# Half of the second weights split before the routing, and the routing table's one-hots on two engines, in an attention and two-MoE kernel

## The chip, the cores and the metric

The kernel runs on one core of a Trainium2 chip. Its time is device time in microseconds of one execution of the whole program. Of the version before there are three timed runs and one profiled execution. All times of a view count from the start of the profiled execution's span.

## What is computed

Three stages in fp32, each feeding the next:

```python
# 1: attention, 2 batches x 8 heads x 768 tokens x 64; a query sees the keys of its own cluster
scores = np.where(mask, scale * np.matmul(q, k.transpose(0, 1, 3, 2)), -1e9)
attn = softmax(scores); x = np.matmul(attn, v)          # then 1536 rows of 512
# 2: a mixture of 8 experts, two experts per row
noisy_logits = x @ w_gate + np.log1p(np.exp(x @ w_noise)) * noise
top2 = np.argpartition(-noisy_logits, 2, axis=1)[:, :2]
h = np.maximum(x[mask] @ w1[e], 0.0)                    # 512 -> 1024
out[mask] += top2_w[mask, k, None] * (h @ w2[e])        # 1024 -> 512
# 3: a second mixture of 8 experts, one expert per row, at most 384 rows each
expert_idx = np.argmax(logits, axis=1)
```

## The kernel before, in words

Everything runs in an order that the program writes out; each engine takes its instructions in that order. Each fp32 operand of a large matmul is split into a high and a low part (fp32r), and three products (high x high, high x low, low x high) make up one. ScalarE makes the high part by a copy, VectorE the low part by a subtraction. A weight half (w1 or w2 of one expert, 512x1024) arrives in four chunks of 512 KB through a staging ring of four buffers; `wload` (L179) queues the chunks, `op` (L199) splits one, `wstep` takes the next in the queue. The first weight half of all is split by ScalarE and GpSimd during attention. High and low part of a half stand in two tiles of a ring of three (`WB`); two of these three pairs are allocated only after attention has given its memory back (L1462).

Attention goes over 16 heads of 6 query tiles. Each head is summed in two halves (`av`, L807): twelve matmuls into one accumulator, which ScalarE then copies to `oT` (L825). `xback` (L829) turns the sums back, scales the rows (L842), writes them to memory, and adds the gate sums `lt` to `LG` (L844, L846).

The experts' work is a list of jobs. Job 0 takes the first expert's rows of batch 0, job 1 the same expert's rows of batch 1, then follow the other experts. A job's first layer is eight groups `wide1` (L1096, f = 0 to 7) of 12 matmuls, each emptied by ScalarE (`hh`, L1108) and VectorE (`hl`, L1109); three accumulators rotate. Its second layer (`second`, L1146) is one pass of 24 matmuls per tile of 128 rows, over eight chunks f. Then the next job's rows, which GpSimd gathers from memory (L1044), are transposed (L1085) and split (L1087, L1088).

Job 0 needs only batch 0. Job 1 needs to know which rows of batch 1 go to the first expert, and that is `route1(1)` (L360): it starts from the complete `LG` (L366), finds the two best experts (mask `A`, L395), sums ranks with small matmuls (`ranks`, L294), turns them to slots (L404 to L314), makes twelve pairs of one-hots (`one_hot`, L318: position `ohp` and value `ohv`, both on VectorE, four buffers each), adds twelve matmuls of them up to a table (L447), and makes the destinations and tokens of it (L449 to L337). Then the gather can be issued. `route1(1)` is a generator that runs beside job 0: at each pause of the job (`tick`, L996) it is advanced by as many steps as the numbers PA and K0 to K3 allow. So its instructions stand between those of job 0, on the same engines. In job 0 a split of the second weights is put behind every second group (L1311).

Of the kernel before, what the change touches and what calls it, by code (L numbers as in the profile page):

```python
# [26 lines left out]
def kernel(  # L27
# [39 lines left out]
    F0, FP, T0, PA = 1, (2, 4), 1.5, 3.0  # L67
    K0, K1, K2, K3 = 10, 3, 1.5, 2
# [104 lines left out]
    WB = [[ring.tile([128, 4096], F32R, name=f"w{p}0") for p in "hl"]]  # L173
# [5 lines left out]
    def wload(n):  # L179
# [5 lines left out]
        for g in range(4):  # L185
# [11 lines left out]
            cs = slice(g * 1024, (g + 1) * 1024)  # L197

            def op(cs=cs, raw=raw, g=g):  # L199
                wh, wl = WB[buf]  # L200
                W[n] = [w.rearrange("p (c f) -> p c f", c=nch) for w in (wh, wl)]
                nc.scalar.activation(wh[:, cs], raw[0], AF.Copy)  # L202
                nc.vector.tensor_tensor(wl[:, cs], raw[0], wh[:, cs].bitcast(F32), op=OP.subtract)  # L203
                clock["out"] -= 1
                wfill()

            def part(half, cs=cs, raw=raw, g=g):
                wh, wl = WB[buf]
                W[n] = [w.rearrange("p (c f) -> p c f", c=nch) for w in (wh, wl)]
                src = raw[0][:, half * 512:(half + 1) * 512]  # L210
                o = slice(cs.start + half * 512, cs.start + (half + 1) * 512)
                nc.scalar.activation(wh[:, o], src, AF.Copy)
                nc.gpsimd.tensor_tensor(wl[:, o], src, wh[:, o].bitcast(F32), op=OP.subtract)
# [146 lines left out]
    def route1(b, psum):  # L360
        LG = LGs[b]
        eng = nc.vector if b else nc.gpsimd
        z = LG[:, :, 8:16]
# [43 lines left out]
        yield  # L407
# [3 lines left out]
        yield  # L411
        t = rt.tile([128, 2, J, E], F32, name="st")
        nc.vector.tensor_tensor(t, oh, rkb[:, None, :, :].to_broadcast([128, 2, J, E]), op=OP.mult)
        yield
        s = rt.tile([128, 2, J], F32, name="ss")
        nc.vector.tensor_reduce(s, t, axis=AX.X, op=OP.add)
        yield
# [5 lines left out]
        yield  # L423
        f = yield from split_slots(s2[:, 0:2].rearrange("p a j -> p (a j)"), 2 * J, "sf")
# [1351 lines left out]
```

## Time and profile before

| what | value |
|---|---|
| timed runs, us | 853.73, 857.37, 858.87 (median 857.37) |
| profiled execution, us | 849.86 |
| its span, us | 848.1 |
| TensorE busy | 820.2 us, 97% |
| TensorE weight loads | 733.6 us, 87% |
| VectorE, ScalarE, GpSimd busy | 540.1, 495.1, 287.9 us |
| mean granted TensorE clock | 0.997 |

The profiled execution's own time is its span and 1.76 us around it. A busy share is a mean over stages with different limits; what a wait costs has to be read in its own stage.

### The profile page before, as it was taken

How to read it: one execution, taken by the hardware profiler on the slowest of the kernel's cores; microseconds unless marked ns; L12 is line 12 of the kernel's file. 1: busy time of each engine (PE TensorE's matmuls, PEld its weight loads, DVE VectorE, ACT ScalarE, POOL GpSimd, SP SyncE). 2: the span in 40 equal slices, each digit the busy share in tenths (PEclk: the TensorE clock that was granted, in tenths of full speed). 3: DMA queues.
4: the chain of work that ended last, by engine and by line, in shares of the span. 5: the costliest groups of instructions: out<-in, count | busy, mean ns of one | idle time of the engine just before them, and what ended most of it. 6: DMA issues, size and time to landing. Idle time of an engine off the chain costs nothing. (4 is left out here: it accounts for less than half of the span.)

```text
span 848.1 us, 14830 instructions
## 1 busy us (share of the span) xinstructions
PE 820.2 (97%) x5350; PEld 733.6 (87%) x5350; DVE 540.1 (64%) x1104; ACT 495.1 (58%) x959; POOL 287.9 (34%) x488
## 2 busy tenths in 40 slices
PE   8999999999998989999999999999999999999997
PEld 6999999888987868989888897988997789888895
DVE  7998888889988666447444443536476548565370
ACT  7989889888888315435343343436254347555461
POOL 3565565667764031231302021124322122222210
PEclk9999999999999999999999999999999999999999
DMA  3125521411113034744644454438465529775250
GB/s 97 34 72 181 198 73 33 147 46 50 39 39 111 20 138 152 241 161 137 185 157 138 166 150 137 119 138 275 144 222 181 191 80 295 274 233 183 87 166 18
DMA packets 62181, 116.75 MB, mean 138 GB/s; under 512 B 13737, under 2 KB 25769, under 8 KB 62096
## 3 DMA queue, kind: packets, MB, share of 16 engines
q1 hardware_dynamic: 52832, 92.60, 34.4%
q0 software_dynamic: 9264, 23.06, 8.1%
q8 instruction: 47, 0.77, 0.4%
q14 instruction: 38, 0.31, 0.1%
HBM read 97.29 MB, written 23.74 MB: 143 GB/s over the span
## 5 line engine op out<-in xcount | busy, mean ns | idle before, releaser
L203 DVE TENSOR_TENSOR wl<-raw,wh 128x1024 fp32r<-128x1024 f32 x124 | 150.3, 1222 | 44.9 <-ACT wh L202 42.5
L1106 PE MATMUL l<-xh,wh 128*128 128x256 f32 (+1 forms) x508 | 156.0, 309 | 2.3 <-ACT xh L1087 0.9
L1106 PE MATMUL l<-xh,wl 128*128 128x256 f32 (+1 forms) x508 | 155.4, 308 | 0.2 <-DVE wl L203 0.2
L1106 PE MATMUL l<-xl,wh 128*128 128x256 f32 (+1 forms) x508 | 148.1, 307 | 0.0
L1151 PE MATMUL l<-wh,hh 128*128 128x512 f32 x328 | 134.9, 411 | 1.5 <-PEq L1343 0.5
L202 ACT ACTIVATE wh<-raw 128x1024 fp32r<-128x1024 f32 x124 | 129.0, 1054 | 7.9 <-DMA raw<-in_moe_w_dram 6.9
L1153 PE MATMUL l<-wh,hl 128*128 128x512 f32 x328 | 129.3, 394 | 0.0
L1152 PE MATMUL l<-wl,hh 128*128 128x512 f32 x328 | 129.0, 393 | 0.0
L1109 DVE SCALAR_TENSOR_TENSOR hl<-l,hh 128x256 fp32r<-128x256 f32 (+1 forms) x127 | 61.3, 484 | 98.6 <-ACT hh L1108 96.4
L1108 ACT ACTIVATE hh<-l 128x256 fp32r<-128x256 f32 (+1 forms) x127 | 55.0, 433 | 101.5 <-PE l L1106 99.6
L801 DVE TENSOR_TENSOR El<-et,Eh 128x384 fp32r<-128x384 f32 x192 | 99.7, 550 | 11.1 <-ACT Eh L800 8.1
L1106 PEld LDWEIGHTS l<-xh,wh 128*128 128x128 f32 x508 | 95.6, 188 | 5.8 <-issue 2.8
L1106 PEld LDWEIGHTS l<-xh,wl 128*128 128x128 f32 x508 | 95.4, 188 | 1.1 <-DVE wl L203 0.4
L769 DVE TENSOR_REDUCE nm<-st 128x1 f32<-128x768 f32 x96 | 91.3, 951 | 6.0 <-PE st L764 4.9
L1106 PEld LDWEIGHTS l<-xl,wh 128*128 128x128 f32 x508 | 93.7, 188 | 0.6
L800 ACT ACTIVATE Eh<-et 128x384 fp32r<-128x384 f32 x192 | 87.2, 493 | 10.5 <-PE et L795 10.2
L778 ACT ACTIVATE E<-st,nm 128x768 f32<-128x768 f32 x96 | 87.1, 907 | 7.6 <-DVE nm L769 7.6
L1195 POOL DMA_INDIRECT y_dram<-y,t1d x23 | 23.2, 1010 | 195.5 <-ACT y L1174 157.5
L1153 PEld LDWEIGHTS l<-wh,hl 128*128 128x128 f32 x328 | 61.6, 188 | 14.9 <-DVE hl L1123 0.3
L1151 PEld LDWEIGHTS l<-wh,hh 128*128 128x128 f32 x328 | 61.8, 188 | 14.6 <-issue 3.1
L795 PE MATMUL et<-identr,Er 128*128 128x128 f32 x576 | 70.9, 241 | 1.1 <-DVE El L801 1.0
L763 PE MATMUL st<-KB,QC 80*128 80x384 f32 x192 | 70.6, 367 | 1.2 <-ACT E L778 1.2
(331 smaller groups left out, 1527.5 us busy)
## 6 DMA issues: line engine op xcount, KB each, us to landing
raw<-in_moe_w_dram SPq DMA_DIRECT2D x128, 512.0 KB, 4.4
vraw<-in_v_dram SPq DMA_DIRECT2D x16, 192.0 KB, 2.5
x_dram<-xp SPq DMA_DIRECT2D x8, 384.0 KB, 3.2
out_dram<-xg SPq DMA_DIRECT2D x1, 3072.0 KB, 9.9
y_dram<-xg SPq DMA_DIRECT2D x1, 3072.0 KB, 9.9
part<-y_dram SPq DMA_DIRECT2D x12, 256.0 KB, 4.2
yt<-y_dram SPq DMA_DIRECT2D x12, 256.0 KB, 4.4
x_dram<-part POOLq DMA_DIRECT2D x12, 256.0 KB, 4.4
```

The lines of the kernel that those rows point to most:

```text
L202: nc.scalar.activation(wh[:, cs], raw[0], AF.Copy)
L203: nc.vector.tensor_tensor(wl[:, cs], raw[0], wh[:, cs].bitcast(F32), op=OP.subtract)
L763: nc.tensor.matmul(ps, st["QC", i][:64 + C, js], st["KB", i][:64 + C, cs], start=True, stop=False)
L769: nc.vector.tensor_reduce(nm, ps, axis=AX.XY, op=OP.max, negate=True)
L778: made = nc.scalar.activation(E, st.pop(("S", i, j))[:, :, :HW], AF.Exp, bias=st.pop(("nm", i, j)), accum_out=st["Z", i][:, j:j + 1])
L795: ins = nc.tensor.transpose(ps[:, n * 128:(n + 1) * 128].bitcast(F32R), E[:, part, n * 128:(n + 1) * 128], identr)
L800: nc.scalar.activation(Eh[o], ps, AF.Copy)
L801: nc.vector.tensor_sub(El[o], ps, Eh[o].bitcast(F32))
L1106: nc.tensor.matmul(ps[:, :n], (w1l if k == 2 else w1h)[:, c, fs], (self.xl if k == 1 else self.xh)[:, c, :n], start=(m == 0), stop=(m == l ...
L1151: nc.tensor.matmul(ps[:rows], hh[:, f, cs], w2h[:, f, :], start=(f == 0), stop=False)
L1152: nc.tensor.matmul(ps[:rows], hh[:, f, cs], w2l[:, f, :], start=False, stop=False)
L1153: nc.tensor.matmul(ps[:rows], hl[:, f, cs], w2h[:, f, :], start=False, stop=(f == FC - 1))
```

## The change

The weight ring's two tiles of a half are cut the other way: tile a holds high and low part of the chunks 0 and 1, tile b those of 2 and 3. The first half-size tile of the second buffer now stands in the ring that exists during attention. So two of the four chunks of job 0's second weights are split before the routing: one before and one behind job 0's first group, which itself is put between the two halves of the last head. The other two are split inside the routing. Job 0's second layer goes by turns (`second_turns`): chunks f 0 to 3 for both tiles, then the twelve table matmuls, then 4 and 5, then 6 and 7. The rank matmuls come after group 5 (`FR`), the routing has fewer pauses, each one-hot has a buffer of its own, and of each pair's second choice ScalarE makes the value: Square of the distance, then Relu of code - 2 code x distance. In the last `xback` the gate sums come before the rows and stay on VectorE.

```diff
-    F0, FP, T0, PA = 1, (2, 4), 1.5, 3.0
-    K0, K1, K2, K3 = 10, 3, 1.5, 2
+    F0, FP, T0, PA, FR = 1, (2, 4), 1.5, 4.5, 5
...
-    WB = [[ring.tile([128, 4096], F32R, name=f"w{p}0") for p in "hl"]]
+    class Half:
+        def __init__(self, tiles, k, nch):
+            self.tiles, self.k, self.per = tiles, k, nch // 2
+        def __getitem__(self, key):
+            _, c, fs = key
+            w = self.tiles[c // self.per][:, self.k].rearrange("p (c f) -> p c f", c=self.per)
+            return w[:, c % self.per, fs]
+    def wtile(pool, p, n):
+        return pool.tile([128, 2, 2048], F32R, name=f"w{p}{n}")
+    WB = [[wtile(ring, p, 0) for p in "ab"], [wtile(ring, "a", 1)]]
...
-                wh, wl = WB[buf]
+                wh, wl = [WB[buf][g // 2][:, p, cs] for p in range(2)]
-                nc.scalar.activation(wh[:, cs], raw[0], AF.Copy)
-                nc.vector.tensor_tensor(wl[:, cs], raw[0], wh[:, cs].bitcast(F32), op=OP.subtract)
+                nc.scalar.activation(wh, raw[0], AF.Copy)
+                nc.vector.tensor_tensor(wl, raw[0], wh.bitcast(F32), op=OP.subtract)
...
-    def one_hot(f, n, code, ncol):
-        oh = rt.tile([128, 128], F32R, name="ohp", bufs=4)
+    def one_hot(f, n, code, ncol, pool=None, minus=None):
+        pool, k = (pool, 2 * J) if pool else (my, 4)
+        oh = pool.tile([128, 128], F32R, name="ohp", bufs=k)
         nc.vector.tensor_scalar(oh, lane, f[:, 0, n:n + 1], None, op0=OP.is_equal)
-        val = rt.tile([128, ncol], F32R, name="ohv", bufs=4)
+        val = pool.tile([128, ncol], F32R, name="ohv", bufs=k)
+        if minus is not None:
+            far = pool.tile([128, ncol], F32, name="far", bufs=2)
+            nc.scalar.activation(far, lane[:, :ncol], AF.Square, scale=-1.0, bias=f[:, 1, n:n + 1])
+            nc.scalar.activation(val, far, AF.Relu, scale=minus, bias=code)
+            return oh, val
...
+        if b:
+            minus = hot.tile([128, J], F32, name="minus")
+            nc.gpsimd.tensor_scalar(minus, code1[:, b, :, 1], -2.0, None, op0=OP.mult)
...
-        if b:
-            yield K0
+        while b and st["f"] < FR:
+            yield
         ps = psum()
         ranks(ps, A, 0)
-        if b:
-            yield K1
...
-            for j in range(J + 1):
-                if j < J:
-                    hots += [one_hot(f, c * J + j, code1[:, b, j, c:c + 1], NC1) for c in range(2)]
-                    yield K2
-                for c in range(2 if j else 0):
-                    n = 2 * (j - 1) + c
-                    nc.tensor.matmul(ps2[:, :NC1], *hots[n], start=(n == 0), stop=(n == 2 * J - 1))
-            yield K3
+            wneed0(1)
+            for j in range(J):
+                hots += [one_hot(f, c * J + j, code1[:, b, j, c:c + 1], NC1, hot, minus[:, j:j + 1] if c else None) for c in range(2)]
+            for n in range(2 * J):
+                while st["pairs2"] < 1:
+                    yield
+                nc.tensor.matmul(ps2[:, :NC1], *hots[n], start=(n == 0), stop=(n == 2 * J - 1))
             nc.vector.tensor_add(st["tab0"], ps2[:, :NC1], st["tab0"])
-            yield
-            st["dst1"], st["tok1"] = yield from finish_table(st["tab0"], "t1", True)
+            st["dst1"], st["tok1"] = drain(finish_table(st["tab0"], "t1", True))
+            wneed0(1)
+            yield
...
+        for part in (gates, rows) if i == NBH - 1 else (rows, gates):
+            part()
...
+        def second_turns(self, hh, hl, pause, before):
+            ps = [p2.tile([128, Dm], F32, name="l2") for _ in self.main]
+            for part, fs in enumerate(((0, 1, 2, 3), (4, 5), (6, 7))):
+                while sum(n == self.h + 1 for n, _, _ in wops) > 2 - part:
+                    wstep()
+                w2h, w2l = W[self.h + 1]
+                for t, rows in self.main:
+                    cs = self.cols(t, rows)
+                    for f in fs:
+                        nc.tensor.matmul(ps[t], hh[:, f, cs], w2h[:, f, :], start=(f == 0), stop=False)
+                        nc.tensor.matmul(ps[t], hh[:, f, cs], w2l[:, f, :], start=False, stop=False)
+                        nc.tensor.matmul(ps[t], hl[:, f, cs], w2h[:, f, :], start=False, stop=(f == FC - 1))
+                        if f % 2 == 1 and f < FC - 1:
+                            if (part, t, f) == (0, 1, 3):
+                                st["pairs2"] = 1
+                            elif (part, t) == (1, 0):
+                                st["pairs2"] = 2
+                            pause()
+                    if part == 2:
+                        y = my.tile([128, Dm], F32, name="y")
+                        nc.scalar.activation(y, ps[t], AF.Copy)
+                        before()
+                        self.scatter(t, rows, y)
+                        pause()
...
-            if (i, t, s) == (NBH, 1, 3):
+            if done[0] == 2 * NBH - 1 and "begun" not in st:
+                st["begun"] = True
                 wneed(0)
+                wneed0(1)
                 for f in range(F0):
                     jobs[0].wide1(f, *st["first"])
+                wneed0(1)
...
-    for n in (1, 2):
-        WB.append([ring3.tile([128, 4096], F32R, name=f"w{p}{n}") for p in "hl"])
+    WB[1].append(wtile(ring3, "b", 1))
+    WB.append([wtile(ring3, p, 2) for p in "ab"])
+    hot = phase["first"].enter_context(tc.tile_pool(name="hot", bufs=1, side="right", reuse_waits="tile"))
```

How the order moves, at three places. First VectorE where attention ends and the routing begins. Before (`hl` is the low part of job 0's first group, `z` the softmax scales, `ra` the routing's first tile):

```order
L801 TENSOR_TENSOR El<-et,Eh 128x3x128 x6
L1109 SCALAR_TENSOR_TENSOR hl<-st,hh 128x256
L832 TENSOR_SCALAR z<-Z 128x6
L833 RECIPROCAL z<-z 128x6
L842 TENSOR_TENSOR xp<-et,z 128x6x64
L844 TENSOR_TENSOR lt<-et,z 128x96
L366 SCALAR_TENSOR_TENSOR ra<-LG_104 128x48
```

Now:

```order
L829 TENSOR_TENSOR El<-et,Eh 128x3x128 x6
L218 TENSOR_TENSOR wa_112<-raw,wa_112 128x1024
L1144 SCALAR_TENSOR_TENSOR hl<-st,hh 128x256
L218 TENSOR_TENSOR wa_112<-raw,wa_112 128x1024
L860 TENSOR_SCALAR z<-Z 128x6
L861 RECIPROCAL z<-z 128x6
L876 TENSOR_TENSOR lt<-et,z 128x96
L878 TENSOR_TENSOR LG_104<-LG_104,lt 128x96
L873 TENSOR_TENSOR xp<-et,z 128x6x64
L390 SCALAR_TENSOR_TENSOR ra<-LG_104 128x48
```

Two weight splits (`wa`) stand ahead of the scales, and the gate sums `lt` and `LG` ahead of the row scaling `xp`.

Second, TensorE at the table matmuls (`ohv`, `ohp` are the one-hots; `l` with a number is a tile's accumulator of the second layer). Before:

```order
L1153 MATMUL l_4977<-wh_4793,hl 128x512
L447 MATMUL rps<-ohv,ohp 128x96 x6
L1151 MATMUL l_4977<-wh_4793,hh 128x512
L1152 MATMUL l_4977<-wl_4794,hh 128x512
L1153 MATMUL l_4977<-wh_4793,hl 128x512
L1151 MATMUL l_4977<-wh_4793,hh 128x512
L1152 MATMUL l_4977<-wl_4794,hh 128x512
L1153 MATMUL l_4977<-wh_4793,hl 128x512
L447 MATMUL rps<-ohv,ohp 128x96 x6
L1151 MATMUL l_5087<-wh_4793,hh 128x512
```

Now:

```order
L1225 MATMUL l_5060<-wa_112,hh 128x512
L1226 MATMUL l_5060<-wa_112,hl 128x512
L475 MATMUL rps<-ohv,ohp 128x96 x12
L1224 MATMUL l_5059<-wb_4798,hh 128x512
L1225 MATMUL l_5059<-wb_4798,hh 128x512
L1226 MATMUL l_5059<-wb_4798,hl 128x512
L1224 MATMUL l_5059<-wb_4798,hh 128x512
L1225 MATMUL l_5059<-wb_4798,hh 128x512
L1226 MATMUL l_5059<-wb_4798,hl 128x512
L1224 MATMUL l_5060<-wb_4798,hh 128x512
```

The two sixes, which stood before and behind the first tile's last two chunks, became one twelve, behind chunks 0 to 3 of both tiles.

Third, VectorE at the one-hots (`sf` holds the slots). Before:

```order
L310 TENSOR_SCALAR si<-si 128x12
L311 TENSOR_SCALAR si<-si 128x12
L314 CAST sf<-si 128x24
L321 TENSOR_SCALAR ohp<-lane,sf 128x128
L323 TENSOR_SCALAR ohv<-lane,sf,code_99 128x96
```

Now:

```order
L325 TENSOR_SCALAR si<-si 128x12
L326 TENSOR_SCALAR si<-si 128x12
L329 CAST sf<-si 128x24
L218 TENSOR_TENSOR wb_4798<-raw,wb_4798 128x1024
L336 TENSOR_SCALAR ohp<-lane,sf 128x128
L344 TENSOR_SCALAR ohv<-lane,sf,code_99 128x96
L336 TENSOR_SCALAR ohp<-lane,sf 128x128 x2
L344 TENSOR_SCALAR ohv<-lane,sf,code_99 128x96
```

A split (`wb`) stands between the slots and the first one-hot, and every second value is gone from VectorE. The two splits that stood ahead of the copy of the ranks (L404) are gone from there; the last of the four now stands behind the token table.

## Rows read from the trace of the kernel before

**Rows 1.** Stage windows: length, TensorE busy (instructions), granted clock, DMA share, GB/s.

```profile
293.57:312.45 18.88, 15.84 (x83) 1.00 0.13 39
312.45:323.95 11.50, 11.50 (x96) 1.00 0.84 302
338.00:450.00 112.00, 111.70 (x558) 1.00 0.54 173
```

**Rows 2.** TensorE timeline: start, us, line, operation [idle before <- releaser].

```profile
278.73 0.44 PE L822 MATMUL acc<-Eh,vt 128*128 128x384 f32 x1 [0.68 <-ACT oT L825]
...
282.40 0.36 PE L1106 MATMUL l<-xh,wh 128*128 128x256 f32 x1
...
290.65 0.39 PE L1106 MATMUL l<-xh,wh 128*128 128x256 f32 x1 [0.59 <-DVE hl L1109]
...
293.57 0.20 PE L298 MATMUL rps<-A,below 128*128 128x48 bf16 x1
...
293.89 0.48 PE L1151 MATMUL l<-wh,hh 128*128 128x512 f32 x1
...
299.40 2.40 PE L447 MATMUL rps<-ohv,ohp 128*128 128x96 f32 x6 [1.07 <-DVE ohv L323]
...
301.64 0.46 PE L1151 MATMUL l<-wh,hh 128*128 128x512 f32 x1
...
303.10 0.54 PE L447 MATMUL rps<-ohv,ohp 128*128 128x96 f32 x4
...
304.51 0.46 PE L1151 MATMUL l<-wh,hh 128*128 128x512 f32 x1
...
310.18 1.34 PE L1085 MATMUL tp<-ident,xg 128*128 128x128 f32 x8
...
312.45 0.39 PE L1106 MATMUL l<-xh,wh 128*128 128x256 f32 x1 [0.92 <-ACT xh L1087]
```

**Rows 3.** VectorE timeline of the same stretch.

```profile
282.64 0.56 DVE L842 TENSOR_TENSOR xp<-et,z 128x384 f32<-128x384 f32 x1 [3.59 <-PE et L836]
...
283.93 0.21 DVE L366 SCALAR_TENSOR_TENSOR ra<-LG 128x48 f32<-128x48 f32 x1 [0.56 <-POOL LG L846]
...
288.20 1.23 DVE L203 TENSOR_TENSOR wl<-raw,wh 128x1024 fp32r<-128x1024 f32 x1
...
293.29 0.21 DVE L395 TENSOR_TENSOR A<-oh 128x48 bf16<-128x48 f32 x1
...
296.68 0.21 DVE L404 COPY rs<-rps 128x56 f32<-128x56 f32 x1
...
298.73 0.29 DVE L321 TENSOR_SCALAR ohp<-lane,sf 128x128 fp32r<-128x128 bf16 x1
...
298.93 0.32 DVE L323 TENSOR_SCALAR ohv<-lane,sf,code 128x96 fp32r<-128x96 bf16 x1
...
304.72 0.26 DVE L449 TENSOR_TENSOR tab<-rps,tab 128x96 f32<-128x96 f32 x1 [0.41 <-PE rps L447]
...
305.57 0.21 DVE L337 TENSOR_SCALAR t1k<-t1d 128x96 int32<-128x96 int32 x1
```

**Rows 4.** ScalarE groups by shape: count, busy us, mean ns, idle before.

```profile
L699 ACT ACTIVATE QC<-et,msc 80x384 fp32r<-80x384 f32 x16 | 9.3, 579 | 0.1
...
L507 ACT ACTIVATE dl<-dl 128x48 f32<-128x48 f32 x2 | 0.5, 244 | 2.4 <-DVE dl L506 2.4
```

**Rows 5.** GpSimd timeline: the first gather for job 1.

```profile
306.06 1.02 POOL L1044 DMA_INDIRECT xg<-x_dram,t1k  x1 [0.83 <-DVE t1k L337]
```

**Rows 6.** Tile xg, 255 to 330 us: gathers from issue to landing.

```profile
DMA to landing us min/median/max: 3.2/4.0/6.0
```

**Rows 7.** TensorE's waits from 312 to 848: total us, times, longest.

```profile
PE l L1106 <- DVE wl L203: 0.2, 1, 0.2
```

**Rows 8.** Stage windows near the start, TensorE; columns as in rows 1.

```profile
15.00:16.00 1.00, 0.17 (x3) 1.00 0.33 66
16.00:20.00 4.00, 3.67 (x20) 0.57 0.44 129
```

More of the change, by code (lines that the diff above doesn't have):

```diff
@@ L207, in part @@
             def part(half, cs=cs, raw=raw, g=g):
-                wh, wl = WB[buf]
-                W[n] = [w.rearrange("p (c f) -> p c f", c=nch) for w in (wh, wl)]
+                W[n] = [Half(WB[buf], p, nch) for p in range(2)]
                 src = raw[0][:, half * 512:(half + 1) * 512]
                 o = slice(cs.start + half * 512, cs.start + (half + 1) * 512)
-                nc.scalar.activation(wh[:, o], src, AF.Copy)
-                nc.gpsimd.tensor_tensor(wl[:, o], src, wh[:, o].bitcast(F32), op=OP.subtract)
+                wh, wl = [WB[buf][g // 2][:, p, o] for p in range(2)]
+                nc.scalar.activation(wh, src, AF.Copy)
+                nc.gpsimd.tensor_tensor(wl, src, wh.bitcast(F32), op=OP.subtract)
                 if half:
@@ L406, in route1 @@
         tot = rs[:, J * E:]
-        yield
+        if not b:
+            yield
         base = eoff1 if b == 0 else st["base"]
@@ L422, in route1 @@
         nc.vector.tensor_tensor(s2[:, 2], s[:, 0], s[:, 1], op=OP.is_lt)
-        yield
-        f = yield from split_slots(s2[:, 0:2].rearrange("p a j -> p (a j)"), 2 * J, "sf")
+        if not b:
+            yield
+        slots = split_slots(s2[:, 0:2].rearrange("p a j -> p (a j)"), 2 * J, "sf")
+        f = drain(slots) if b else (yield from slots)
         if b == 0:
@@ L841, in xback, with rows, gates @@
         r = z[:, 1][:, :, None]
-        nc.vector.tensor_tensor(xp[:, :, h % 2, :], acc[:, :, 0:D], r.to_broadcast([128, J, D]), op=OP.mult)
         lt = LG if h == 0 else wk.tile([128, J, 16], F32, name="lt")
-        nc.vector.tensor_tensor(lt, acc[:, :, D:], r.to_broadcast([128, J, 16]), op=OP.mult)
-        if h:
-            nc.gpsimd.tensor_tensor(LG, LG, lt, op=OP.add)
+        def rows():
+            nc.vector.tensor_tensor(xp[:, :, h % 2, :], acc[:, :, 0:D], r.to_broadcast([128, J, D]), op=OP.mult)
+        def gates():
+            nc.vector.tensor_tensor(lt, acc[:, :, D:], r.to_broadcast([128, J, 16]), op=OP.mult)
+            if h:
+                (nc.vector if i == NBH - 1 else nc.gpsimd).tensor_tensor(LG, LG, lt, op=OP.add)
+        for part in (gates, rows) if i == NBH - 1 else (rows, gates):
+            part()
         if h % 2 == 1:
@@ L1310, in work @@
                 job.wide1(f, hh, hl)
-                if job is jobs[0] and f % 2 == 0:
-                    wneed0(1)
+                if job is jobs[0]:
+                    st["f"] = f
                 tick(12 * job.n / 2400, PA if job is jobs[0] else 3.0)
@@ L1315, in work @@
             rest = job.tile1(0, hh, hl, tick, fill)
-        wneed(job.h + 1)
+        if job is not jobs[0]:
+            wneed(job.h + 1)
         early()
@@ L1324, in work @@
         wfill()
-        for t, rows in job.main:
+        if job is jobs[0]:
+            job.second_turns(hh, hl, step, early)
+            early()
+            fill(False)
+            fill(False)
+        for t, rows in job.main if job is not jobs[0] else ():
             if t and t == len(job.main) - 1 and job.tail:
@@ L1608 @@
     st["rush"] = True
+    st["f"] = st["pairs2"] = 0
     spawn(route1(1, mpsum))
@@ L1727, in after_last @@
         ring4 = pool("split", "ring4")
-        WB.append([ring4.tile([128, 4096], F32R, name=f"w{p}3") for p in "hl"])
+        WB.append([wtile(ring4, p, 3) for p in "ab"])
         P["split"] = (128, pool("split", "mxs"), pool("split", "mhs"))
```

13 lines of the change are left out of this document (8 added, 5 removed).

## The prediction

> **What bounds the kernel now.** I read the stage windows first, then TensorE's timeline between attention and the second job, then VectorE's timeline in the same stretch. In the long middle of the program TensorE works 111.70 of 112.00 us [rows 1], so a microsecond saved on another engine there is worth nothing. TensorE is also the engine that sets the end: a microsecond in which it stands still is paid in full, wherever it is. The stretch that the change rewrites is a place where it stands still often: from 282.40, where the first job's second matmul group starts, to 312.45, where the second job starts [rows 2], 30.05 us.
>
> What the reader is to see there, in TensorE's order. At 278.73 the weighted sum of the last half head waits 0.68 us for ScalarE to empty the accumulator. The seven remaining first-layer groups take 11.17 us; the second job does eight such groups in 11.50 us, 1.44 each, without a gap [rows 1], so seven should take 10.06 and 1.11 are lost, 0.59 of them in the wait at 290.65 for VectorE [rows 2]. Then the rank matmuls at 293.57 (0.32 us). Then second-layer matmuls, 24 of which run from 304.51 to 310.18, that is 0.236 each; 18 from 293.89 should end at 298.14. But the next one starts at 301.64: 3.50 us go to six table matmuls that VectorE feeds one one-hot at a time. The other six cost 1.41 (303.10 to 304.51). Last, eight transposes and the wait for the copied rows: 310.18 to 312.45, 2.27 us, 0.92 of it idle [rows 2].
>
> VectorE's timeline says why: the routing of batch 1 is a chain on it, from the gate sums at 283.93 to the token table at 305.57 [rows 3], and four weight splits of 1.23 us (one stands as 288.20) lie between its links. TensorE is served whatever is ready and then waits.
>
> **The change, part by part.** Times below are those of the profiled execution; a place in the changed kernel is called its clock.
>
> *End of attention.* The first group of job 0 now stands between the two half heads. The accumulator is emptied while it runs, so the 0.68 us [rows 2] and the restart behind it go, which I put at 0.2: **0.9 us less** (0.7 to 1.0). Two weight splits are put ahead of the last accumulator copy on ScalarE and of the softmax scales on VectorE. Each costs VectorE 1.23 [rows 3]. I cost them at nothing: VectorE waited 3.59 us at 282.64 for TensorE, which covers both, and on ScalarE they lie beside job 0's group (1.44) and the matmuls of the last half head. If that cover were gone the routing would start late by what exceeds it.
>
> *Gate sums.* On VectorE, ahead of the row scaling, instead of GpSimd behind it. Before, routing began 1.29 us after the first of these operations (282.64 to 283.93). Now it is two short operations and the 0.56 us scaling, some 0.95. With the 0.9 above the routing starts at about 282.7, 1.2 earlier.
>
> *First-layer groups.* With two splits out of the routing's chain, VectorE empties the accumulators in time. Of the 1.11 us I leave 0.2: **0.9 less** (0.5 to 1.1).
>
> *Ranks after group 5.* The chain from the gate sums to the mask A took 283.93 to 293.50 [rows 3], 9.57, with two splits of 1.23 inside and one accumulator operation that now comes later (a few tenths): some 6.9 remain, so A is there at 289.6. TensorE reaches the ranks at 281.5 + 5 x 1.44 + 0.2 = 288.9. **A new wait of 0.7** (0 to 1.5, the upper end if one split's worth of chain is left). Queued behind it are groups 6 and 7, which wait for nothing else.
>
> *One-hots.* Ranks end at 290.0, groups 6 and 7 at 292.9, and 24 second-layer matmuls (four chunks, both tiles) at 292.9 + 5.67 = 298.6. VectorE: the rank copy at 290.5; from there to the first one-hot 2.05 us (296.68 to 298.73) and the third split 1.23: 293.8. Twelve position one-hots at 0.20 (298.73 to 298.93) and six values at 0.32 or less [rows 3]: ready at 298.1. ScalarE makes the other six values, two operations each. No row has a 128x96 operation of this kind; the nearest are 0.244 (48 wide, fixed scale) and 0.579 (384 wide with a per-row scale) [rows 4], so a pair lies between 0.49 and 1.16, and six from 292.5 end between 295.4 and 299.5. I take 0.8, as 96 is nearer to 48 and two operands are per row: 297.3. Both are done before TensorE asks at 298.6. Then the twelve run together: four cost 0.54 where they were ready [rows 2], 0.135 at most and 0.08 without the last one's tail; I take 0.11, 1.3 us. Before 3.50 + 1.41, now 1.3: **3.6 less** (3.3 to 3.9, and up to 0.9 worse if ScalarE takes the upper end).
>
> The Trainium skill speaks against this edit ("ScalarE: Activation LUTs", Rules for kernel authors): simple multiplies and maxima belong on VectorE. Per value the rows bear it out, 0.8 against 0.32. Weighed as a whole it does not decide: twelve pairs on VectorE alone would end at 293.8 + 12 x 0.52 = 300.0 instead of 298.1, and TensorE would wait 1.4. Kept to the rule, the sum would be -2.5; I go by the rows.
>
> *Second layer by turns.* Same 48 matmuls, same price. Both tiles need only half the weights until 298.6; the third split is done at 293.8 and the fourth, behind the token table (300.1 + 1.06, 304.72 to 305.78 in [rows 3], + 1.23), at 302.4, ahead of its use at 299.9 + 12 x 0.236 = 302.7. Nearly no margin, at most 0.5 of wait, which would only stand in the next one's place.
>
> *Rows of batch 1.* The table addition starts 0.21 after the last table matmul's successor (304.51 to 304.72), the gather 1.34 after that (306.06) [rows 2, 3, 5], and rows land 4.0 after issue in the median, 3.2 to 6.0 [rows 6]. Now: matmuls free at 299.9, table at 300.1, gather 301.4, landed 305.4. TensorE has 18 matmuls (4.25 us) left before it wants them: 304.15. **A new wait of 1.3** (0.4 to 3.3). The output scatter of the first tile now stands behind the two gathers in GpSimd's queue; nothing of this stage waits for it.
>
> *Transposes.* One tile's transposes and copy now lie beside six matmuls of the other tile: **0.5 less** than 2.27 (0 to 0.9).
>
> *Weights in two tiles.* Same bytes, same splits, same order of transfers. Later waits for a split sum to 0.2 us [rows 7]. Nothing.
>
> The sum: -0.9 - 0.9 + 0.7 - 3.6 + 1.3 - 0.5 = **-3.9 us**. With all good ends it is -6.4, with all bad ends about +1. Against the profiled 849.86 that is 846.0. The timed runs were longer, 853.73 to 858.87 with median 857.37, 7.5 above the profiled one; the changed kernel should be timed likewise: **853.5**.
>
> **Rivals.**
>
> *More is won.* A is ready when TensorE comes and the rows land in 3.2: both new waits nearly vanish, -5.5 to -6.4, about 851.5. For it: the chain has been cleared of two splits. Against it: 4.0 is the median landing, and the last group's margin is short.
>
> *The rows eat it.* ScalarE's pairs cost 1.16 and the gather lands after 6.0: +0.9 and +2.0, leaving 1.0: 856.4. For it: the row of 0.579. Against it: the 6.0 is one of eight.
>
> *It is given back.* The second job starts earlier but the third job's weights do not, so TensorE waits there: no change, 857.4. It would need transfers that set the pace. Against it: the window 338 to 450 has 0.3 us without TensorE work [rows 1], and the next weights are issued behind the same gather, which moves ahead by as much.
>
> *The clock falls, and it gets slower.* From 15 to 16 us TensorE worked 0.17 us, and from 16 to 20 the granted clock was 0.57 in the mean, the lower level of 1.2 GHz for most of it [rows 8]; that costs 0.43 x 4 = 1.7 us. The changed stage has three waits of this order (0.7, 1.3 and the 0.9 before the second job). If each is followed by such a fall, 5.1 us are lost: +1.2, 858.6. It turns the sign from the third fall on (3.9 / 1.7 = 2.3). Against it: the idle 1.07 at 299.40 and 0.92 at 312.45 stand in windows with clock 1.00 [rows 1, 2]. The Trainium skill ("TensorE: Matmul & The Clock Gate", What's actually happening) says that the lower clock is the default and activity releases it; the 16 to 20 row agrees, and by that rule every new wait is a risk.
>
> **How the numbers follow.** My forecast (-3 to -5) 0.58, more won 0.13, eaten 0.17, given back 0.08, clock 0.04. The remaining sign of error is the runs themselves: three runs lie from 3.6 under their median to 1.5 over it. The range runs from 853.5 less 2.5 for the better case and 3.5 for the runs, 847.5, to the eaten and given-back cases and 1.1 of run spread, 858.5. One per cent, about what a measurement here tells from no change, is 8.6 us. No case wins that much, so faster by more than it needs the run spread too: 0.08. Slower by more than it needs the clock case and more: 0.03. Within: 0.89.
>
> **What would show it.** Right: between the last half heads no wait for the accumulator; twelve table matmuls in one row without a wait; the token table near 301 instead of 305.57; the second job's first matmul near 308.5. Wrong: a wait over 1.5 us at the ranks (chain term), a wait for ScalarE at the table matmuls (pair term), over 2 us at the first transposes (landing term), a granted clock under 1.00 between 282 and 312, or a new wait for weights in the second or third job.

## The result, and the profile after

| | before | after |
|---|---|---|
| median of timed runs, us | 857.37 (853.73 to 858.87) | 846.65 (846.2 to 850.65) |
| profiled execution, us | 849.86 | 846.2 |
| its span, us | 848.1 | 844.4 |

The ratio is 0.9896, with a 95% interval from 0.9873 to 0.9918: about 1% faster, where 0.45% was forecast (five timed runs of each). From profiled execution to profiled execution the gain is 3.7 us, where the prediction's sum was 3.9. The timed runs gained 10.7. So the two numbers have to be explained apart.

First the traces. The stage windows of the changed kernel (columns as in [rows 1]): the stretch from the ranks to the second job, the second job's first layer, and the middle.

```profile
290.07:309.12 19.05, 16.98 (x104) 1.00 0.17 45
309.12:321.00 11.88, 11.88 (x98) 1.00 0.85 289
334.00:446.00 112.00, 111.70 (x559) 1.00 0.54 173
```

The middle is what it was, 111.70 of 112. TensorE's timeline shows the places that the prediction spoke of:

```profile
278.26 0.33 PE L850 MATMUL acc<-Eh,vt 128*128 128x384 f32 x1
...
281.83 0.36 PE L1141 MATMUL l<-xh,wa 128*128 128x256 f32 x1
...
290.07 0.20 PE L313 MATMUL rps<-A,below 128*128 128x48 bf16 x1 [0.56 <-DVE A L419]
298.86 1.44 PE L475 MATMUL rps<-ohv,ohp 128*128 128x96 f32 x12
305.90 0.66 PE L1120 MATMUL tp<-ident,xg 128*128 128x128 f32 x4 [1.34 <-DMA xg<-x_dram,t1k]
...
309.12 0.39 PE L1141 MATMUL l<-xh,wa 128*128 128x256 f32 x1 [0.74 <-ACT xh L1122]
```

The wait of 0.68 between the half heads is gone. The twelve table matmuls, which were spread over 299.40 to 304.51 [rows 2], are one group without a wait. Two new waits stand there, 0.56 at the ranks and 1.34 for the gathered rows. VectorE's timeline, which answers to [rows 3]:

```profile
289.80 0.21 DVE L419 TENSOR_TENSOR A<-oh 128x48 bf16<-128x48 f32 x1
...
290.59 0.21 DVE L426 COPY rs<-rps 128x56 f32<-128x56 f32 x1
...
293.74 0.28 DVE L336 TENSOR_SCALAR ohp<-lane,sf 128x128 fp32r<-128x128 bf16 x1
...
297.34 0.28 DVE L336 TENSOR_SCALAR ohp<-lane,sf 128x128 fp32r<-128x128 bf16 x1
...
300.33 0.26 DVE L476 TENSOR_TENSOR tab<-rps,tab 128x96 f32<-128x96 f32 x1 [1.87 <-PE rps L475]
...
301.17 0.21 DVE L358 TENSOR_SCALAR t1k<-t1d 128x96 int32<-128x96 int32 x1
```

The mask A was forecast at 289.6 and came at 289.80; the first one-hot at 293.8, came at 293.74; the table at 300.1, came at 300.33. On ScalarE a value takes two operations. The first two pairs start 0.84 us apart, the later ones 0.76 to 0.77, where 0.8 was assumed (start, length, line, operation):

```profile
292.64 0.38 ACT L341 ACTIVATE far<-lane,sf 128x96 f32<-128x96 bf16 x1 [1.77 <-DVE sf L329]
293.11 0.47 ACT L342 ACTIVATE ohv<-far,code,minus 128x96 fp32r<-128x96 f32 x1
293.48 0.36 ACT L341 ACTIVATE far<-lane,sf 128x96 f32<-128x96 bf16 x1
```

And GpSimd's gather, issued at 301.4 by the forecast, with its landing over the first jobs' rows ([rows 5, 6]):

```profile
301.65 1.81 POOL L1079 DMA_INDIRECT xg<-x_dram,t1k  x1 [20.30 <-DVE t1k L358]
```

```profile
DMA to landing us min/median/max: 3.0/4.2/5.9
```

### The profile page after: what moved, and what is told of

It is laid out like the page before. It is cut to its first block, busy times and chain, and to the rows that moved or that the text cites. A ratio compares the mean times of both kernels' runs of the same rounds, so it can differ in the third digit from the quotient of the medians.

```text
span 844.4 us, 14848 instructions
## 1 busy us (share of the span) xinstructions
PE 817.8 (97%) x5350; PEld 733.4 (87%) x5350; DVE 539.2 (64%) x1099; ACT 499.4 (59%) x971; POOL 288.1 (34%) x488
## 5 line engine op out<-in xcount | busy, mean ns | idle before, releaser
L1141 PE MATMUL l<-xh,wa 128*128 128x256 f32 (+1 forms) x508 | 126.0, 311 | 1.5 <-ACT xh L1122 0.7
L1141 PE MATMUL l<-xh,wb 128*128 128x256 f32 (+1 forms) x508 | 125.0, 308 | 0.2 <-DVE wb L218 0.2
L218 DVE TENSOR_TENSOR wa<-raw,wa 128x1024 fp32r<-128x1024 f32 x62 | 75.9, 1226 | 36.4 <-ACT wa L217 34.1
L1141 PEld LDWEIGHTS l<-xh,wa 128*128 128x128 f32 x508 | 89.0, 188 | 5.1 <-issue 2.8
L1141 PEld LDWEIGHTS l<-xh,wb 128*128 128x128 f32 x508 | 88.9, 188 | 0.6 <-DVE wb L218 0.4
L218 DVE TENSOR_TENSOR wb<-raw,wb 128x1024 fp32r<-128x1024 f32 x62 | 75.1, 1221 | 10.6 <-ACT wb L217 10.6
L1141 PE MATMUL l<-xl,wb 128*128 128x256 f32 (+1 forms) x254 | 75.7, 307 | 0.0
L1141 PE MATMUL l<-xl,wa 128*128 128x256 f32 (+1 forms) x254 | 75.5, 307 | 0.0
L217 ACT ACTIVATE wa<-raw 128x1024 fp32r<-128x1024 f32 x62 | 65.3, 1053 | 4.1 <-DMA raw<-in_moe_w_dram 3.3
L848 PE MATMUL acc<-El,vt 128*64 128x384 f32 x192 | 66.9, 351 | 0.0
```

Of the source, the lines that this page charges most:

```text
L217: nc.scalar.activation(wh, raw[0], AF.Copy)
L218: nc.vector.tensor_tensor(wl, raw[0], wh.bitcast(F32), op=OP.subtract)
L848: nc.tensor.matmul(acc[:64, :HW], vt[:, 0], El[:, t], start=False, stop=(t == J - 1), skip_group_check=True)
L1141: nc.tensor.matmul(ps[:, :n], (w1l if k == 2 else w1h)[:, c, fs], (self.xl if k == 1 else self.xh)[:, c, :n], start=(m == 0), stop=(m == l ...
```

## The measure that the experiments go by

All runs below are on other occasions than the first ones; the kernel before takes 855 to 866.5 us in the median on them, so every kernel is compared with the runs of before that stand beside it. In the traces I use one stretch: from the first of the last head's 24 weighted-sum matmuls (both of its halves) to the second job's first matmul. It holds the whole change. The expectations call it "from the last half head to the second job", or the stage. Before it runs from 271.62 to 312.45, 40.83 us; after from 271.97 to 309.12, 37.15.

| kernel | the stretch in each trace, us | traces with a granted clock under 1.00 in it |
|---|---|---|
| before (first trace, e0, e6, e7, e11) | 40.83, 44.45, 43.37, 44.54, 44.73 | 4 of 5 |
| before, values on ScalarE (e8) | 44.67 | 1 of 1 |
| before, waits filled (e2, e10, e12, e14, e15) | 40.86, 40.86, 40.95, 40.84, 40.85 | 0 of 5 |
| after (first trace, e1, e4, e16) | 37.15, 37.22, 37.20, 37.18 | 0 of 4 |
| after, values on VectorE (e5) | 37.14 | 0 of 1 |
| after, ranks later (e13, e17) | 36.76, 36.69 | 0 of 2 |
| after, table starved (e3) | 38.40 | 1 of 1 |
| after, late splits (e9) | 39.90 | 1 of 1 |

## Experiments: was it the occasion, or the clock?

Clock theory: in most executions of the kernel before, the granted clock falls to its lower level (1.2 GHz, 0.50 in the rows) behind the waits for the one-hots; I call this a fall. The first trace is an exception. The change takes away these waits, and so the falls. Rivals: the first comparison was a chance of the occasion, or the longer runs come from another stage.

**e0, e1: both kernels again.** No edit.

> The kernel before, unchanged, to see how its timed executions differ from its profiled one (849.86 us against a median of 857.37). Theory clock: its timed executions lose 4 to 9 us to falls of TensorE's granted clock that the profiled one was spared; then executions near 857 show a mean granted clock of 0.985 to 0.992, those near 850 show 0.997. Theory chip: the earlier timed executions were on a slower occasion; then it is timed at 849 to 851 here with a clock of 0.996 to 0.997. Theory memory: long executions with a clock of 0.997, lengthened by transfers.

> The changed kernel, unchanged, beside the kernel before. Theory clock: 846 to 848 us at a clock of 0.996, ratio about 0.989 as long as the kernel before shows its falls. Theory chip: ratio 0.9955 (the 3.7 us that the two profiles differ by). Theory memory: 846 to 848 and a ratio of about 0.989 without a difference in clock.

Against the kernel before in the same rounds e0 has 1.0003 (0.9973 to 1.0034) and e1 0.9908 (0.9874 to 0.9942). The gain is not a chance of the occasion, though it is 6.2 us here where it was 10.7. Both are slower than expected: 868.08 and 860.33 us in the median, at mean clocks of 0.984 and 0.988, where I had e1 at 846 to 848 and 0.996. The trace of e0 has a fall inside the stage.

**e6, e7, e11: the kernel before, more traces.** No edit.

> The kernel before, nothing edited, for a second trace of the clock. Clock theory: the granted clock falls to the lower level between the one-hot wait and the second job's first matmul, as in one of the two traces so far (3.6 us more from the last half head to the second job than the 40.83 us of the trace without a fall). Rival: no fall there, 40.8 us, and the longer time comes from other stages.

> As the run before it, a third trace: clock theory 42.5 to 45 us from the last half head to the second job with a granted clock under 1.00 there; rival 40.8 us at clock 1.00. Of three to four traces of this kernel the clock theory wants at least half with a fall.

> The kernel before, one more trace on the chip of the filled one. Clock theory: a fall between 300 and 320, 42.5 to 45 us from the last half head to the second job; rival: 40.8.

All three have the fall. In e7, stage windows of TensorE and its timeline:

```profile
302.00:306.00 4.00, 2.60 (x9) 0.83 0.00 0
306.00:310.00 4.00, 4.00 (x13) 0.50 0.00 0
310.00:314.00 4.00, 4.00 (x10) 0.50 0.33 94
314.00:318.00 4.00, 4.00 (x17) 0.89 0.41 93
```

```profile
303.48 2.53 PE L447 MATMUL rps<-ohv,ohp 128*128 128x96 f32 x6 [1.09 <-DVE ohv L323]
305.81 0.76 PE L1151 MATMUL l<-wh,hh 128*128 128x512 f32 x1
306.37 0.63 PE L1152 MATMUL l<-wl,hh 128*128 128x512 f32 x1
306.80 0.63 PE L1153 MATMUL l<-wh,hl 128*128 128x512 f32 x1
```

TensorE waits 1.09 us and is then fed six table matmuls over 2.3 us, as in the first trace (1.07 and 2.24, [rows 2]). Here the clock falls while it is being fed. The second-layer matmuls behind it stand 0.43 us apart instead of 0.236, and the stretch is 3.7 us longer than in the first trace. Over the four traces with a fall it is 2.5 to 3.9 us longer.

**e2, e10, e12, e14, e15: the waits filled.** In the kernel before, small matmuls into a spare accumulator stand ahead of the table matmuls whose one-hots are late. Nothing else moves.

```diff
+    FILL = {0: 4, 2: 3, 4: 3, 10: 1}
...
+    def fillers(n):
+        pp = pt.tile([128, DC, 128], F32, name="tp")
+        for _ in range(n):
+            nc.tensor.matmul(pp, onesb, lane[:, None, :].to_broadcast([128, DC, 128]), start=True, stop=True)
...
+                    if n in FILL:
+                        fillers(FILL[n])
                     nc.tensor.matmul(ps2[:, :NC1], *hots[n], start=(n == 0), stop=(n == 2 * J - 1))
```

> The kernel before, with small bf16 matmuls into a spare accumulator put into TensorE's waits for the one-hots: 4 ahead of the first table matmul, 3 ahead of the third and of the fifth, 1 ahead of the eleventh, 0.21 us each by 512 columns. They fill waits of 1.07, about 0.8, 0.8 and 0.28 us, nothing else moves, and the output is the same. Clock theory (the waits at the one-hots let the granted clock fall to the lower level in many executions of the kernel before, at about 3.4 us a time): the stage 282 to 312 shows clock 1.00, and the timed median lies 2 to 4 us below the kernel before in the same rounds, mean clock up by 0.003 to 0.006. Rival (the long runs come from elsewhere, transfers or other stages): the median stays within 1 us of before, or rises by up to 1 us where a filler is still running when its one-hot is ready.

> The kernel before with TensorE's waits at the one-hots filled with small matmuls, a second time. Clock theory: no fall in the stage in its trace (40.8 us from the last half head to the second job), and a median 2 to 3.5 us below the kernel before (3.6 us a fall, in three of four executions), mean clock up by 0.003. Rival: the median within 1 us of before at the same mean clock, so that the fall does not hang on these waits or is made good by another one later.

> The filled kernel, one more trace. Clock theory: no fall, 40.8 us; rival: a fall as often as in the kernel before, three of four, 42.5 to 45 us.

> The filled kernel, a further trace. If the filling keeps the clock up in the stage: 40.8 to 40.9 us from the last half head to the second job, falls elsewhere or none. If it only makes the fall rarer or the traces so far were luck: a fall between 300 and 320 and 42.5 to 45 us.

> The filled kernel, the last of its traces: 40.8 to 40.9 us at clock 1.00 in the stage if the filling keeps the clock up, 42.5 to 45 us with a fall there if it does not.

In e10, windows of the stretch and TensorE's timeline:

```profile
298.00:302.00 4.00, 3.78 (x20) 1.00 0.00 0
302.00:306.00 4.00, 3.82 (x20) 1.00 0.13 49
306.00:310.00 4.00, 4.00 (x20) 1.00 0.42 129
```

```profile
297.91 1.04 PE L365 MATMUL tp<-lane,onesb 128*128 128x512 bf16 x4
299.11 0.66 PE L456 MATMUL rps<-ohv,ohp 128*128 128x96 f32 x2 [0.16 <-DVE ohv L324]
299.61 0.82 PE L365 MATMUL tp<-lane,onesb 128*128 128x512 bf16 x3
300.08 0.56 PE L456 MATMUL rps<-ohv,ohp 128*128 128x96 f32 x2
```

The table takes as long as before, TensorE only does something meanwhile, and the stretch stays at 40.84 to 40.95 in five of five traces, all at clock 1.00. With the waits open, five of six traces have a fall (e8 among them). That is what the clock theory expects, but the filled traces weigh less than it seems. Between 570 and 620 us, in a stage that neither the change nor the filling touches, the clock falls too in twelve of the twenty traces. The window in the first trace of before, in e7 and in e2:

```profile
570.00:620.00 50.00, 48.52 (x387) 1.00 0.61 200
570.00:620.00 50.00, 45.48 (x303) 0.97 0.53 177
570.00:620.00 50.00, 45.80 (x286) 0.90 0.50 164
```

All five traces with the waits open and a fall in the stretch have this later fall as well; the first trace of before has neither. Of the filled traces e10, e12, e14 and e15 have neither, so their executions might have been spared in the stretch without fillers too. Only e2 has the later fall and none in the stretch. That the filling keeps the clock up rests on this one trace and is not shown. For the change itself the traces say more: e1, e4, e16 and e5 all have the later fall, and none has one in the stretch.

The timing does not bear the filling out to the full either. The medians are 864.06 against 864.96 (0.9988, 0.9965 to 1.0011) and 854.1 against 855.29 (0.9987, 0.9962 to 1.0012), 0.9 and 1.2 us less, where the traces would give 43.58 in the mean of before less 40.87, 2.7. Both intervals reach that far, but they hold no gain at all as well. Of the twelve runs of e10 five have a mean clock of 0.998 or 0.999 and take 849.8 to 851.4, seven have 0.986 to 0.991 and take 853.5 to 857.4. Of the 23 runs of before beside them four are over 0.996: a smaller share, but these are too few runs to show a difference. More than half of the filled runs lose clock all the same. Where they lose it is not shown, as they have no traces. The later fall is a candidate: from the second job's first matmul to the end of the span the eight traces without it take 535.3 to 536.4 us, the twelve with it 539.4 to 544.3.

**e3: the wait put back.** The changed kernel, table matmuls behind 6 second-layer matmuls instead of 24.

```diff
-                            if (part, t, f) == (0, 1, 3):
+                            if (part, t, f) == (0, 0, 1):
                                 st["pairs2"] = 1
```

> The changed kernel with its twelve table matmuls put behind 6 of the second layer's matmuls instead of behind 24, so that TensorE waits there for one one-hot after the other, as it did before the change. TensorE comes at 292.9 + 1.4 = 294.3, the last one-hot is ready at 298.1, so the table ends at 298.3 with 18 second-layer matmuls still to do (4.25 us) where the changed kernel ends it at 300.1 with none: +2.4; the gathered rows come 1.9 earlier and TensorE comes 1.5 earlier to them: -0.3. Waits alone (rival): +2.1 us against the changed kernel in the same rounds, with the same mean clock. Clock theory: +3.5 to +6 us in the median, since such a starved stretch is followed by a fall of the granted clock in a good part of the executions; mean clock lower by 0.002 to 0.006.

TensorE is fed one one-hot at a time again, 3.39 us for the group, and the clock falls behind it (windows, then the row):

```profile
300.00:304.00 4.00, 3.82 (x13) 0.81 0.00 0
304.00:308.00 4.00, 4.00 (x14) 0.76 0.30 73
```

```profile
298.88 3.39 PE L475 MATMUL rps<-ohv,ohp 128*128 128x96 f32 x12
```

The stretch is 1.2 us longer than in the changed kernel, less than the 2.1 that I worked out from waits alone. The table takes 1.95 us more (298.88 to 302.10 against 1.27). The waits of 1.34 for the rows and of 0.74 ahead of the second job are gone. The fall makes the nine second-layer matmuls behind the table some 1.4 us longer (302.10 to 305.73 against 9 x 0.236), but costs next to nothing in this trace, since TensorE's weight load then still waits for the rows; without the fall it would have waited longer:

```profile
308.06 0.42 PEld L1120 LDWEIGHTS tp<-ident,xg 128*128 128x128 f32 x4 [0.43 <-DMA xg<-x_dram,t1k]
```

The median, 860.81 (ratio 0.9946, 0.9921 to 0.9972), is 3.1 above the changed kernel in the same rounds, where the clock theory had 3.5 to 6, and the mean clock over its runs is 0.989 against 0.9925. The direction is that of the clock theory; the intervals of the two overlap, and the 1.9 us beyond the stretch are not explained by the trace.

**e4, e16: the changed kernel beside them.** No edit.

> The changed kernel, nothing edited, beside the others on the same chip. Both theories: 0.99 of the time before (7 to 9 us less). Clock theory: its runs have a higher mean clock than those of the kernel before, by 0.003 or more, and at equal clock only 4 to 5.5 us of the gain are left; rival: equal clocks, all of the gain at every clock.

> The changed kernel, nothing edited. By the traces 3.7 us of waits, and by the clock another 1 to 4: 4.7 to 7.7 us less than before (ratio 0.991 to 0.9945), mean clock higher by 0.002 or more. Without a clock term (rival): 3.7 us, ratio 0.9957, equal clocks.

Ratios 0.9909 (0.9877 to 0.9941) and 0.9933 (0.9908 to 0.9958). Mean clocks 0.9925 against 0.987 for before, and 0.993 against 0.9895. Within one kernel's runs on one occasion a hundredth of mean clock goes with about 5 us (a line through the runs of e0 to e16, before and after each about its own mean on each occasion), so 2.9 and 1.7 of the gains of 7.3 and 4.7 us go with the clock. On the occasion of e16 the rest is 3.0, near the 3.7 of the waits; on that of e4 it is 4.4. (For e1 it is 6.2 us, 0.988 against 0.985: 1.7 with the clock and 4.5 besides.)

## Experiments: the terms of the sum

**e5, e8: the values on ScalarE.** e5 is the changed kernel without this part, e8 the kernel before with this part alone.

```diff
-                hots += [one_hot(f, c * J + j, code1[:, b, j, c:c + 1], NC1, hot, minus[:, j:j + 1] if c else None) for c in range(2)]
+                hots += [one_hot(f, c * J + j, code1[:, b, j, c:c + 1], NC1, hot) for c in range(2)]
```

> The changed kernel with all twelve values of the one-hots made on VectorE, as before; ScalarE's Square and Relu are gone. By the prediction's working the twelve pairs end at 293.7 + 12 x 0.52 = 300.0 and TensorE waits 1.4 at the table matmuls. Rival: only the last pairs are late, since the first of them are ready when TensorE comes at 298.9 and each table matmul waits for its own pair alone; then the last one starts at 300.0 instead of 300.0 and the loss is 0 to 0.3 us. Timed: +1.4 or +0.2 us against the changed kernel; the profile's wait at the table matmuls decides.

> The kernel before with this part of the change alone: of each pair's second choice ScalarE makes the value (Square, then Relu). VectorE's time per two pairs falls from 0.88 to 0.64 us, but ScalarE needs 0.8 for its value, so the pitch falls by 0.08 a time and six times 0.08 = 0.5 us less at the table is the most; the stage from the last half head to the second job 40.3 to 40.8 us where the clock is 1.00. Rival (the prediction's own weight on this part): 1.4 us less, 39.4.

TensorE in e5, and the last one-hots on VectorE there:

```profile
307.53 1.44 PE L475 MATMUL rps<-ohv,ohp 128*128 128x96 f32 x12
```

```profile
306.95 0.36 DVE L344 TENSOR_SCALAR ohv<-lane,sf,code 128x96 fp32r<-128x96 bf16 x1
307.19 0.32 DVE L336 TENSOR_SCALAR ohp<-lane,sf 128x128 fp32r<-128x128 bf16 x1
307.39 0.36 DVE L344 TENSOR_SCALAR ohv<-lane,sf,code 128x96 fp32r<-128x96 bf16 x1
```

No wait, and the stretch is 37.14: this part of the change is worth nothing. Timed 0.9908 against e4's 0.9909. My 1.4 had two errors. A pair on VectorE takes 0.44 us, not 0.52: of the 0.20 and 0.32 that I added, the first is the step from one start to the next, the second the length of an operation, whose next neighbour starts 0.24 behind it. And twelve matmuls that each wait for their own pair need only the last one late. The rule of the Trainium skill that I weighed ("ScalarE: Activation LUTs", Rules for kernel authors: such simple operations on VectorE) would have cost nothing here. The traces agree with it: a value takes 0.24 us on VectorE, 0.76 to 0.84 on ScalarE.

In e8 ScalarE sets the pace, and TensorE waits for it:

```profile
306.02 0.85 PE L455 MATMUL rps<-ohv,ohp 128*128 128x96 f32 x3 [1.05 <-DVE ohv L328]
307.24 0.42 PE L455 MATMUL rps<-ohv,ohp 128*128 128x96 f32 x2 [0.37 <-ACT ohv L326]
308.14 0.45 PE L455 MATMUL rps<-ohv,ohp 128*128 128x96 f32 x1 [0.48 <-ACT ohv L326]
```

The first six matmuls take from 306.02 to about 308.4, as long as before. The trace has a clock fall in it, so the size of 0.5 can't be read; a gain of 1.4 is not there.

**e9: the early splits undone.** Both splits stand behind the groups 2 and 4 again.

```diff
                 wneed(0)
-                wneed0(1)
                 for f in range(F0):
                     jobs[0].wide1(f, *st["first"])
-                wneed0(1)
...
                     st["f"] = f
+                    if f in (2, 4):
+                        wneed0(1)
```

> The changed kernel with the two early splits of the second weights undone: they stand behind the groups 2 and 4 again, among the routing's links on VectorE. The prediction's working: the mask A comes 2 x 1.23 = 2.5 later, the wait at the ranks grows from 0.56 to about 3.0, and the stage from the last half head to the second job from 37.15 to 39.2 to 39.7 us. Rival: the chain has slack elsewhere (the wait for the gathered rows is set by the table, which TensorE asks for at its own time), then less than 1 us. Clock theory besides: the longer wait brings clock falls of their own, so that the timed median rises by more than the stage does.

```profile
299.20 0.20 PE L313 MATMUL rps<-A,below 128*128 128x48 bf16 x1 [1.71 <-DVE A L419]
```

```profile
300.00:304.00 4.00, 4.00 (x24) 0.57 0.00 0
```

```profile
295.68 1.22 DVE L218 TENSOR_TENSOR wa<-raw,wa 128x1024 fp32r<-128x1024 f32 x1
...
298.94 0.21 DVE L419 TENSOR_TENSOR A<-oh 128x48 bf16<-128x48 f32 x1
...
299.40 1.22 DVE L218 TENSOR_TENSOR wa<-raw,wa 128x1024 fp32r<-128x1024 f32 x1
```

The wait at the ranks is 1.71 and not 3.0. Of the two splits only one comes ahead of the mask A on VectorE; the other stands behind it, so A comes 1.1 us later and not 2.5. Behind the wait the clock falls; in the kernel before TensorE does not wait at the ranks [rows 2]. The longer wait, 1.1, and 1.6 behind the ranks, where the fall is, make the stretch 39.90. The median is about that of before, 865.12 against 864.79, 0.9983 (0.9948 to 1.0019); the changed kernel was not timed on this occasion, and has 0.990 to 0.993 on others. Of the parts that I undid (the values on ScalarE in e5, the place of the table matmuls in e3, the early splits here) this one costs the stretch most: 2.7 us, against none and 1.2.

**e13, e17: the ranks behind group 6.**

```diff
-    F0, FP, T0, PA, FR = 1, (2, 4), 1.5, 4.5, 5
+    F0, FP, T0, PA, FR = 1, (2, 4), 1.5, 4.5, 6
```

> The changed kernel with the rank matmuls behind group 6 instead of group 5. The wait at the ranks (0.56 us) goes; the ranks end 0.9 later, the one-hots are ready at 298.5 instead of 297.6, and TensorE asks at 298.3: no wait or 0.2. The stage from the last half head to the second job 36.6 to 36.9 us instead of 37.15 to 37.2, which the timing cannot tell from no change against the changed kernel (0.991 of before). Rival: the later chain makes the table's last one-hots late, and the stage stays at 37.2 or grows to 37.6.

> The changed kernel with the ranks behind group 6, beside the changed kernel itself: 0.3 to 0.5 us less by the stage (36.76 against 37.15 to 37.2 from the last half head to the second job), which is below what these rounds can tell; both theories, medians within 1.5 us of each other.

```profile
290.89 0.20 PE L313 MATMUL rps<-A,below 128*128 128x48 bf16 x1
298.30 1.44 PE L475 MATMUL rps<-ohv,ohp 128*128 128x96 f32 x12
305.42 0.66 PE L1120 MATMUL tp<-ident,xg 128*128 128x128 f32 x4 [1.42 <-DMA xg<-x_dram,t1k]
```

The wait at the ranks is gone, no other one has come, and the stretch is 36.76 and 36.69: 0.4 to 0.5 us better than the change, as worked out. e13 has 0.9941 (0.9916 to 0.9966) against before, with no changed kernel beside it. e17 has 0.9924 (0.9896 to 0.9952), the changed kernel beside it 0.9933, which the runs can't tell apart. By the traces it is the shortest version here.

## Why the prediction was wrong, step by step

*What bounds the kernel, and the terms.* Right in the main. The wait at the accumulator and the restart: 0.9 forecast, 0.92 measured (from the last head to the second group, 10.78 to 9.86). The new wait at the ranks: 0.7, measured 0.56. The one-hots: twelve matmuls in 1.3, measured 1.27 (298.86 to 300.13), so 3.6 gained. The wait for the gathered rows: 1.3, measured 1.34. The first-layer groups gained 0.6 where I had 0.9 (11.17 before; now 281.83 to 290.07 less the 0.56, and 290.38 to 293.27). From the end of the table to the second job TensorE spends 2.0 us besides its 24 matmuls and the wait for the rows (309.12 less 298.86, 1.27, 24 x 0.236 and 1.34), where it was 2.27, so 0.3 was gained where I had 0.5. The stretch as a whole is 3.68 shorter, where the sum was 3.9. (All good ends of the sum make -6.5, not the -6.4 that stands there; nothing hangs on it.)

*A right term for a wrong reason.* The time of the one-hots was right, its division was not: ScalarE's values add nothing (e5).

*The step that failed* is the last one of the sum: "The timed runs were longer ... 7.5 above the profiled one; the changed kernel should be timed likewise". The changed kernel's median lies 0.45 above its profiled execution, which is one of its five timed runs. On the later occasions the median lies anywhere from 5.8 us under the profiled execution to 4.2 over it: one profiled execution is a single draw. And the gap of 7.5 was itself, in part, a cost of the stage that I was costing. All four later traces of the kernel before have a fall of the granted clock in that stage; the one that I had read has none. By the traces, the mean stretch goes from 43.58 to 37.19, 6.4 us, of which 3.7 are waits and 2.7 falls. The later medians gained 6.2, 7.3 and 4.7 us.

The stage is not all of the gap. The four later traces of before have spans 8.7 to 19.5 us longer than the first one; 2.5 to 3.9 of that lie in the stretch, 0.8 to 8.3 ahead of it and 4.0 to 8.6 behind it. The later traces of the changed kernel lose alike ahead and behind (0.7 to 9.3 and 4.1 to 7.9), and nothing in the stretch.

On the first occasion the gain was 10.7, and the 4 us beyond the 6.4 are not explained by any trace that I have. With 6.4 the time would have been 851, inside the range. The five timed runs of the changed kernel have mean clocks of 0.993 to 0.997 there, where its runs have 0.988, 0.9925 and 0.993 in the mean on later occasions, so part of it may be luck, few falls in these five runs. The clocks of the runs of before on that occasion are not on record, and the point stays open.

*The rival of the clock* had the mechanism and put it on the wrong side. I charged falls to the changed kernel's new waits and gave the old ones none, "Against it: the idle 1.07 at 299.40 and 0.92 at 312.45 stand in windows with clock 1.00". That is one execution, and it was the exception. The price was too low as well: 1.7 us a fall there, 2.5 to 3.9 by the traces of before. The wait of 1.3 to 1.4 us for the rows has been followed by clock 1.00 in all eight traces that have it. *More is won* had the size of the first timing for a reason that did not happen: both new waits are there. *The rows eat it* and *given back* did not happen: the pairs took 0.76 to 0.84, the rows landed after 4.2 in the median, and the third job's transposes start as much earlier as the second job (322.02 instead of 325.34).

*The range* ended at 847.5, with the runs' own spread as its lower margin; 846.65 is below. Chances of 0.08 for a gain over 1% followed from the same step: with no falls to lose in the kernel before, no case could win so much.

## What to carry to other kernels

When timed runs lie well above the profiled execution, the gap is no constant to carry over: ask which stage makes it, and take a second and third trace of the kernel as it is before costing a change to a stage in which TensorE is fed in small pieces. A wait costs its own length while the clock holds, and more where a fall follows (2.5 to 3.9 us here). And take the pitch of a run of operations from their starts, not from the length of one.

## What the runs showed of the hardware that was not expected

The length of a wait alone does not tell whether the clock falls behind it. Waits of 1.05 to 1.09 us with thin feeding behind them, small matmuls one after the other as their one-hots came, brought a fall in five of six traces. The wait of 1.32 to 1.42 for the rows, with dense work ahead of it (4.00 of 4.00 us from 298 to 302 in the first trace of after), brought none in eight, the wait of 1.71 at the ranks in e9 a fall in the one trace that has it. Elsewhere a wait of 1.40 in the attention, at 222.92 in e4, is followed by one:

```profile
222.92 0.97 PE L864 MATMUL et<-RW,oT 128*128 128x80 f32 x6 [1.40 <-ACT oT L853]
```

```profile
222.00:226.00 4.00, 3.08 (x17) 0.70 0.00 0
```

That wait is not in the first traces. The kernel before takes 855.3 us in the median on the occasion of e10 and 865.0 on that of e2, at mean clocks of 0.990 and 0.987, too near each other for 10 us at 5 us a hundredth. In the traces the last head begins at 271.3 to 272.4 us on the one and at 276.2 to 280.6 on the other, and from the second job to the end of the span 535.9 to 539.7 us pass on the one and 541.4 to 544.3 on the other. Both kernels have it alike, and its cause was not looked for.

A fall cost less than the clock lost in it: in e7 some 10 us at half clock (the four windows lack 1.28 x 4 = 5.1 us of full clock) made the stretch 3.7 us longer, not 5. Part of them lie in 302 to 306, where TensorE was busy 2.60 of 4.00 us and had time to lose. In e3 a fall of some 1.4 us cost next to nothing, because TensorE would have waited for the rows instead.
